# Spreading side work evenly through an attention window, and moving relayout DMAs to another queue

## The chip, the cores and the metric

The kernel runs on one core of a Trainium2 chip. The metric is the device time of one execution in microseconds (us). The trace is of one profiled execution; its span is about 2 to 3 us shorter than the time measured for the same run.

## The reference

CSWin attention over an image of 224 x 224 tokens with 96 channels. A projection gives q, k and v. The first 48 channels attend inside 28 horizontal stripes of 8 rows, the last 48 inside 28 vertical stripes of 8 columns; a stripe ("window" here) has 1792 tokens. Then comes an output projection. Cut to what matters:

```python
qkv = jnp.einsum('bhwc,cd->bhwd', x, wqkv)            # x (1,224,224,96), wqkv (96,288), bfloat16
qh = q[..., :C2].reshape(B * nh, sw * W, C2)          # 28 horizontal windows, C2 = 48
ah = _softmax(jnp.einsum('bqc,bkc->bqk', qh, kh) * scale, axis=-1)
oh = jnp.einsum('bqk,bkc->bqc', ah, vh).reshape(B, H, W, C2)
# the same over 28 vertical windows, with transposes before and after, gives ov
o  = concat(oh, ov)                                   # written with two pads and a sum
return jnp.einsum('bhwc,cd->bhwd', o, wo)
```

## The kernel before

The kernel writes one program per engine. A window is 25 groups: 24 of two 128x512 score tiles, each followed by one 128x1024 exp on ScalarE (ACT), and one half group. The score matmuls of group G wait until exp has freed the PSUM banks of group G-2, so PE and ACT share two PSUM buffers. The products with V (PV) follow two or three groups later.

Everything else PE has to do for a window is a queue of "side items": four transposes of x, eight q and k projections and two of v, 14 in all, for the next window; in vertical windows also four transposes (ot) and four output projections (fin). After every even group, two items are taken from the queue. PE's program has its work in this order.

```python
        while True:
            cur_slot["G"] = G
            if G < NG:
                g = groups[G]
                if g["first_of_win"]:
                    ...                               # load x of window wid + 2
                    if wid + 1 < NWIN:
                        enqueue_proj(wid + 1)         # 14 items
                emit_st(G)                            # scores on PE, exp on ACT
            if G % 2 == 0 or G >= NG:
                for Gp in (G - 3, G - 2):
                    if 0 <= Gp < NG and Gp not in pv_cnt:
                        emit_pv(Gp)
                emit_from(2)                          # two side items, while there are any
            G += 1
```

The DMAs between the two layouts go through DRAM. POOL issues them and waits for each; SP issues the loads and stores. The weights arrive in one tile, and POOL copies them into padded ones.

```python
        def pool_dma(out_ap, in_ap):
            pool.wait(pq_sem, pq_sem.cnt)             # one relayout at a time
            return dma(pool, pq_sem, out_ap, in_ap)

        dma(act, w_sem, wst[:, :], wqkv[:, :])
        dma(act, w_sem, wo_sb[:, :], wo[:, :])
        pool.wait(w_sem, c_w)
        ...                                           # ten tensor_copy on POOL: wst -> wq, wk, wv
        c_pool_const = pool.op(lambda e: e.memset(sigt[:, 0:1], 1.0), sig=True)   # PE waits for this
        ...
        src = xf[L * w: L * (w + 1)].rearrange("(b p) c -> p b c", p=128)         # x rows of 192 B
```

At the change from horizontal to vertical (the "transition"), the last horizontal result goes to DRAM, is relaid out there, and comes back as Ocomb, for which the first ot item waits.

The softmax here doesn't subtract the row's maximum and nothing guards it: scores larger than these inputs give would overflow.

## Time and profile before

Median 1359.84 us over five runs (1357.71 to 1361.52). The profiled run spans 1356.8 us.

| what | before |
|---|---|
| ACT busy | 1280.4 us, 94% |
| PE busy | 1134.5 us, 84% |
| exp: idle before it, ended by PE | 62.8 us |
| DMA share | about 22% |
| one horizontal window | 24.07 us |
| one undisturbed vertical window | 22.91 us |
| recorded time at half PE clock | 245 us in 28 stretches |

From the page of the kernel before: busy time of each engine; then, over 40 equal slices, busy tenths of ACT and the PE clock that was granted, also in tenths; then the shares of the chain that ended last.

```profile
PE 1134.5 (84%) x16918; PEld 617.0 (45%) x16918; DVE 586.8 (43%) x1456; ACT 1280.4 (94%) x1401; POOL 56.1 (4%) x141
...
ACT  5999999999999999999989999999999999999996
PEclk9887898899889788888967999999999989999998
...
ACT 81%; PE 17%; DMA 1%; issue 1%; DVE 0%; POOL 0%; ACTq 0%; POOLq 0%; DVEq 0%
```

ACT sets the time, and the chain says so too. But the horizontal half, the left half of the slices, has clocks of 7, 8 and 9 tenths where the vertical half has 9 nearly throughout.

Next, the largest groups of instructions of the kernel before: line, engine, operation, output from input, count | busy us, mean ns | idle time before, and what ended it.

```profile
L525 ACT ACTIVATE PT<-ps 128x1024 bf16<-128x1024 f32 x1344 | 1251.6, 1055 | 64.9 <-PE ps L514 62.8
L514 PE MATMUL ps<-QT,KT 49*128 49x512 bf16 (+1 forms) x3136 | 571.9, 389 | 207.1 <-ACT PT L525 196.0
...
L126 POOL DMA_DIRECT2D oh_scratch<-oh_scratch x28 | 18.8, 673 | 593.2 <-DMA oh_scratch<-O_sb 593.2
L126 POOL DMA_DIRECT2D out_dram<-out_scratch x28 | 15.4, 549 | 634.3 <-DMA out_scratch<-out_sb 612.5
```

Of the 64.9 us in which ACT stood before an exp, PE's scores ended 62.8. POOL's relayouts have 593 and 613 us of waiting ahead of them, but the chain that ended last puts 0% of the span down to POOL.

Where the idle time lies is seen in ACT's own timeline, here from the kernel before around one end of a horizontal window (start us, length us, what, [idle before <- what ended it]).

```profile
205.78 1.94 ACT L525 ACTIVATE PT<-ps 128x1024 bf16<-128x1024 f32 x2 [0.20 <-PE ps L514]
207.61 0.60 ACT L527 ACTIVATE PT<-ps 128x512 bf16<-128x512 f32 x1
208.42 1.02 ACT L525 ACTIVATE PT<-ps 128x1024 bf16<-128x1024 f32 x1 [0.21 <-PE ps L514]
210.64 1.94 ACT L525 ACTIVATE PT<-ps 128x1024 bf16<-128x1024 f32 x2 [1.20 <-PE ps L514]
213.07 1.94 ACT L525 ACTIVATE PT<-ps 128x1024 bf16<-128x1024 f32 x2 [0.49 <-PE ps L514]
```

The stretch view of the same place in the kernel before has the clock: stretch, its length, busy us of PE, PEld, DVE, ACT and POOL, granted PE clock, DMA share, GB/s.

```profile
202.00:203.00 1.00, 0.98 (x20) 0.63 (x20) 0.00 (x0) 1.00 (x2) 0.00 (x0) 1.00 0.05 16
203.00:204.00 1.00, 0.47 (x6) 0.13 (x4) 0.00 (x0) 1.00 (x2) 0.00 (x0) 0.90 0.00 0
204.00:206.00 2.00, 2.00 (x28) 0.98 (x24) 0.00 (x0) 1.80 (x3) 0.00 (x0) 0.50 0.00 0
...
212.00:214.00 2.00, 2.00 (x24) 1.10 (x23) 1.02 (x2) 1.50 (x3) 0.00 (x0) 0.50 0.13 21
214.00:216.00 2.00, 1.90 (x31) 0.93 (x28) 1.29 (x2) 2.00 (x4) 0.67 (x1) 0.99 0.21 32
```

The rest follows from the order of emission. Fourteen items at two per even group are gone after seven even groups; in the second half of a horizontal window PE has only scores and PV. Depending on how that falls on the grid, a grid window comes out low enough for a drop (in the 19 drops of the horizontal phase the grid window before had PE busy for 0.677 to 0.715). The next attention window then begins with two items per even group at half clock, and there PE can't keep up with ACT: from 212 to 214 us PE is busy for 2.00 us of 2.00, ACT for 1.50.

### The profile page before, as it was taken

The page shows a single profiled execution, that of the slowest core. Times are in us where ns is not written, and L with a number is a line of the kernel's source. Part 1 is how long each engine was busy: PE and PEld are TensorE (multiplying, and loading weights), DVE is VectorE, ACT ScalarE, POOL GpSimd, SP SyncE. Part 2 cuts the span into 40 slices and gives each one's busy share as a digit, 9 for nine tenths or more (in the row PEclk, how much of TensorE's full clock was granted, in tenths as well). Part 3 has the DMA queues.
Part 4 walks back from the last instruction along what each step waited for, and adds up shares of the span by engine and source line. Part 5 has one row for each costly group of instructions (what it writes and reads, how often), then busy time and mean ns, then how long its engine had stood idle before and what let it go on. Part 6 is the DMA issues. An engine that isn't in the chain of part 4 may idle for free.

```text
span 1356.8 us, 37466 instructions
## 1 busy us (share of the span) xinstructions
PE 1134.5 (84%) x16918; PEld 617.0 (45%) x16918; DVE 586.8 (43%) x1456; ACT 1280.4 (94%) x1401; POOL 56.1 (4%) x141
## 2 busy tenths in 40 slices
PE   7888878878887888888889888888888888888886
PEld 3444444444444444444445444444444444444443
DVE  3443333424334343343434555555554545455552
ACT  5999999999999999999989999999999999999996
POOL 1000000000000000000000000000000000000000
PEclk9887898899889788888967999999999989999998
DMA  2221222212122221222222222222222222222211
GB/s 36 45 49 33 49 46 44 49 39 56 34 49 47 43 49 34 50 44 45 50 43 50 57 54 57 53 54 48 56 54 55 50 53 57 52 55 53 57 33 34
DMA packets 263408, 65.07 MB, mean 48 GB/s; under 512 B 257512, under 2 KB 257608, under 8 KB 263248
## 3 DMA queue, kind: packets, MB, share of 16 engines
q1 hardware_dynamic: 255872, 38.56, 16.5%
q0 software_dynamic: 7152, 24.04, 6.1%
q8 instruction: 132, 2.16, 0.7%
q14 instruction: 28, 0.23, 0.1%
q10 hardware_dynamic: 224, 0.07, 0.0%
HBM read 48.19 MB, written 38.49 MB: 64 GB/s over the span
## 4 chain that ended last, share of the span: by engine, by line
ACT 81%; PE 17%; DMA 1%; issue 1%; DVE 0%; POOL 0%; ACTq 0%; POOLq 0%; DVEq 0%
ACT PT L525 80%; PE ps L514 7%; PE ps L560 5%; PE ps L274 2%; PE ps L299 1%; PE ps L348 1%; ACT PT L527 0%; DMA Ocomb<-oh_scratch 0%; DMA oh_scratch<-oh_scratch 0%; DMA wo_sb<-in_wo_dram 0%; PE ps L375 0%; DVE KT L307 0%; DMA out_scratch<-out_sb 0%; DMA oh_scratch<-O_sb 0%; DVE QT L307 0%
## 5 line engine op out<-in xcount | busy, mean ns | idle before, releaser
L525 ACT ACTIVATE PT<-ps 128x1024 bf16<-128x1024 f32 x1344 | 1251.6, 1055 | 64.9 <-PE ps L514 62.8
L514 PE MATMUL ps<-QT,KT 49*128 49x512 bf16 (+1 forms) x3136 | 571.9, 389 | 207.1 <-ACT PT L525 196.0
L560 PEld LDWEIGHTS ps<-VA,PT 128*128 128x128 bf16 x10976 | 347.5, 99 | 193.6 <-issue 183.7
L560 PE MATMUL ps<-VA,PT 128*128 128x49 bf16 x10976 | 426.2, 190 | 0.9 <-DVE VA L330 0.6
L514 PEld LDWEIGHTS ps<-QT,KT 49*128 49x128 bf16 x3136 | 137.5, 95 | 521.5 <-ACT PT L525 427.3
L581 DVE RECIPROCAL rl<-ps 128x4 f32<-128x4 f32 x224 | 40.3, 180 | 357.9 <-PE ps L560 357.9
L307 DVE CAST QT<-ps 128x512 bf16<-128x512 f32 x224 | 135.7, 617 | 64.6 <-PE ps L299 64.6
L307 DVE CAST KT<-ps 128x512 bf16<-128x512 f32 x224 | 138.4, 618 | 25.2 <-PE ps L299 25.0
L281 DVE COPY xT<-ps 96x512 bf16<-96x512 bf16 x224 | 84.8, 382 | 69.0 <-PE ps L274 68.7
L355 DVE COPY OTs<-ps 96x512 bf16<-96x512 bf16 x112 | 43.4, 387 | 122.1 <-PE ps L348 122.1
L274 PE MATMUL ps<-ident,xin 128*96 128x128 bf16 x784 | 92.9, 253 | 0.0
L383 DVE CAST out_sb<-ps 128x384 bf16<-128x384 f32 x112 | 56.7, 506 | 79.7 <-PE ps L375 79.2
L299 PE MATMUL ps<-xT,wk 96*128 96x512 bf16 x224 | 83.6, 373 | 2.1 <-POOL sigt L154 1.2
L274 PEld LDWEIGHTS ps<-ident,xin 128*96 128x96 bf16 x784 | 72.8, 149 | 7.1 <-issue 4.6
L299 PE MATMUL ps<-xT,wq 96*128 96x512 bf16 x224 | 75.9, 361 | 0.0
L330 DVE CAST VA<-ps 128x384 bf16<-128x384 f32 x112 | 56.2, 502 | 28.7 <-PE ps L321 28.7
L348 PE MATMUL ps<-ident,Ocomb 128*96 128x128 bf16 x392 | 44.7, 234 | 1.9 <-DMA Ocomb<-oh_scratch 1.9
L126 POOL DMA_DIRECT2D oh_scratch<-oh_scratch x28 | 18.8, 673 | 593.2 <-DMA oh_scratch<-O_sb 593.2
L597 DVE TENSOR_TENSOR O_sb<-ps,rl 128x192 bf16<-128x192 f32 x112 | 37.3, 333 | 11.9 <-DVE rl L581 0.5
L126 POOL DMA_DIRECT2D out_dram<-out_scratch x28 | 15.4, 549 | 634.3 <-DMA out_scratch<-out_sb 612.5
L597 DVE TENSOR_TENSOR Ocomb<-ps,rl 128x192 bf16<-128x192 f32 x112 | 37.2, 332 | 3.9
L321 PE MATMUL ps<-wv,xT 96*128 96x48 bf16 x784 | 37.9, 184 | 0.5 <-DVE xT L281 0.5
(28 smaller groups left out, 224.3 us busy)
## 6 DMA issues: line engine op xcount, KB each, us to landing
x_scratch<-in_x_dram POOLq DMA_DIRECT2D x28, 336.0 KB, 3.4
xin<-x_scratch SPq DMA_DIRECT2D x28, 336.0 KB, 3.8
xin<-in_x_dram SPq DMA_DIRECT2D x27, 336.0 KB, 3.8
out_dram<-out_scratch POOLq DMA_DIRECT2D x27, 336.0 KB, 3.2
out_scratch<-out_sb SPq DMA_DIRECT2D x84, 96.0 KB, 1.9
oh_scratch<-oh_scratch POOLq DMA_DIRECT2D x28, 168.0 KB, 2.8
Ocomb<-oh_scratch SPq DMA_DIRECT2D x28, 168.0 KB, 2.8
oh_scratch<-O_sb SPq DMA_DIRECT2D x84, 48.0 KB, 1.8
```

The lines of the kernel that those rows point to most:

```text
L274: c = pe.op(lambda e, bb=bb, blk=blk, bank=bank, s=s: e.transpose(psb[0:96, 1024 * bank + 128 * bb: 1024 * bank + 128 * (bb + 1)], xin[s][ ...
L281: cd = dve.op(lambda e, bank=bank, b=b, q0=q0, wdt=wdt: e.tensor_copy(xT[b][:, q0:q0 + wdt], psb[0:96, 1024 * bank: 1024 * bank + wdt]), s ...
L299: c = pe.op(lambda e, bank=bank, b=b, q0=q0, wdt=wdt, wmat=wmat: e.matmul(ps[:, 512 * bank: 512 * bank + wdt], wmat[:, :], xT[b][:, q0:q0 ...
L307: cd = dve.op(lambda e, bank=bank, dst=dst, q0=q0, wdt=wdt: e.tensor_copy(dst[:, q0:q0 + wdt], ps[:, 512 * bank: 512 * bank + wdt]), sig=True)
L330: cd = dve.op(lambda e, bank=bank, b=b, blk0=blk0, nb=nb: e.tensor_copy(VA[b][:, blk0: blk0 + nb, 0:48], ps[:, 512 * bank: 512 * bank + 48 ...
L348: c = pe.op(lambda e, bank=bank, qb=qb, vb=vb, j=j: e.transpose(psb[0:96, 1024 * bank + 128 * qb: 1024 * bank + 128 * (qb + 1)], Ocomb[vb] ...
L355: cd = dve.op(lambda e, bank=bank, vb=vb, q0=q0, wdt=wdt: e.tensor_copy(OTs[vb][:, q0:q0 + wdt], psb[0:96, 1024 * bank: 1024 * bank + wdt] ...
L383: cd = dve.op(lambda e, bank=bank, vb=vb, j=j, nqb=nqb: e.tensor_copy(out_sb[vb][:, 4 * j:4 * j + nqb, :], ps[:, 512 * bank: 512 * bank + ...
L514: c = pe.op(lambda e, base=base, bk=bk, col=col, width=width, rt=rt, i=i, b=b, q0=q0: e.matmul(ps[:, base + 512 * bk + col: base + 512 * b ...
L525: ca = act.op(lambda e, base=base, pt=pt: e.activation(pt[:, 0:1024], ps[:, base:base + 1024], ACTF.Exp, scale=scale), sig=True)
L560: c = pe.op(lambda e, obank=obank, jj=jj, pt=pt, pcol=pcol, qb=qb, b=b, i=i, st=st: e.matmul(ps[:, 512 * obank + 64 * jj: 512 * obank + 64 ...
L597: c2 = dve.op(lambda e, so=so, nqb=nqb, oview=oview, dst=dst: e.tensor_tensor(dst, oview[:, :, 0:48], rl[so][:, 0:nqb].unsqueeze(2).broadc ...
```

## The change

Its summary names DMAs: move the relayout DMAs from POOL to SP, load the weights into their padded tiles directly, put the horizontal relayouts off by a window so that SP doesn't block. The diff has two further parts: x rows are laid out so that a partition reads 2688 contiguous bytes in horizontal windows, and the number of side items per even group is computed. One warm-up matmul is added too. Its core, cut:

```diff
-KNOBS = dict(nwh=28, nwv=28, warm=6, dummies=0)
+KNOBS = dict(nwh=28, nwv=28, warm=7, dummies=0)
...
-        dma(act, w_sem, wst[:, :], wqkv[:, :])
-        ...                                          (ten POOL copies)
+        for d0 in (0, 64):
+            dma(act, w0_sem, wk[0][:, d0:d0 + 48], wqkv[:, 96:144])
+        for d0 in (0, 64):
+            dma(act, w0_sem, wq[0][:, d0:d0 + 48], wqkv[:, 0:48])
+        dma(act, w0_sem, wv[0][:, :], wqkv[:, 192:240])
...
-            return dma(pool, pq_sem, out_ap, in_ap)
+            return dma(sp, rq_sem, out_ap, in_ap)
...
-                    src = xf[L * w: L * (w + 1)].rearrange("(b p) c -> p b c", p=128)
+                srcw = xf[L * w: L * (w + 1)].rearrange("(p b) c -> p b c", b=NKB)
...
                 if j == 3:
-                    pool_after_hwin(wid)
+                    if w == NWH - 1:
+                        flush_pending_hwin()
+                        sp_after_hwin(wid)
+                    else:
+                        pending_hwin.append(wid)     (flushed after chunk 0 of the next window)
...
-                emit_from(2)
+                if G < NG:
+                    gl = G % NGW
+                    even_left = max(1, (NGW - gl + 1) // 2)
+                    nelig = sum(1 for ent in queue if ent[2] <= G)
+                    k = (nelig + even_left - 1) // even_left
+                    k = max(1, min(3, k))
+                else:
+                    k = 2
+                emit_from(k)
```

The last hunk shares the waiting items out over the even groups left in the window: in a horizontal window 2,(2),1,1,...,1 in place of 2,2,2,2,2,2,2,0,0,0,0,0.

## The prediction

> **What bounds the kernel.** ScalarE. The page's busy table gives ACT 1280 of 1357 us (94%); the chain of waits runs 80% over the exp (ACT PT). Back to back, a 128x1024 exp takes 0.927 us, a window (24 and a half one) 22.9 us. ACT's timeline shows 24.07 us per window in the horizontal phase (39.8 to 689.7 us, 27 windows), but 22.91 in clean vertical windows. The surplus is ACT waiting for PE ps L514.

> **Why PE is late.** The stretch view shows PEclk falling to 0.50 28 times, 244 us in all, in whole multiples of 3.41 us on one fixed grid. [...] On that grid nearly every full-clock window with PE busy below about 0.71 is followed by a drop (27 drops, busy 0.57 to 0.715; 296 kept windows average 0.83). Before emits two side items (transposes, projections) per even group until the 14 of a horizontal window are gone; from group 14 on PE has only scores and PV (1.35 us busy per 1.84 us pair, 0.73), on the threshold. About every second window drops (203.8 to 214.0 us), and the next window's front-loaded items run at half clock: ACT loses 0.2+0.2+1.2+0.5 us.

> **What the change does, by worth.**
> 1. Adaptive emission. Counting through the queue: horizontal windows go from 2,2,2,2,2,2,2,0,0,0,0,0 to 2,(2),1,1,1,...,1. One item (0.36 to 0.40 us) per pair lifts PE to about 0.85. Horizontal drops should nearly vanish: 27 x (24.07 - 22.91) = 31 us. In the vertical phase the empty slots at window ends are filled too; drops there cost about 6.8 us, I count 5.5.
> 2. Transition (690 to 744 us): two windows take 54.2 instead of 45.8 us: a drop on entry, 1.85 us of PE waiting for Ocomb, then seven low-clock grid windows. The change removes the entry drop (1.9 us) but keeps the chain store, relayout, Ocomb load, now with the last x relayout inside the wait. I expect a stall of about 2 us again, and half clock after it: 2 us net.
> 3. Relayouts from POOL to SP: the POOL waits (612 and 593 us) are off the critical path; DMA is at about 22%. [...] about 0, with SP not blocking loads because the waits are deferred a window. Contiguous x rows (2688 rather than 192 B) cut packets: about 0 too.
> 4. Direct weights: removes copies ending at 5.5 us (PE waited 1.2 us for sigt); five ACT issues at 0.47 us plus 2.4 us landing give an estimated 5.2 us; one more warm matmul (0.43 us) delays the transposes. Net within 0.5 us.

> Sum: 31 + 5.5 + 2 = 38.5 us, all on the critical path.

> **Predicted:** 1321 us, range 1312 to 1338. Faster by over 2%: 0.86, within 2%: 0.12, slower: 0.02.

> **What would show it right:** 22.9 to 23.0 us per horizontal window; mean PEclk from 0.91 to about 0.98; low stretches from 244 us to under 60, mostly around the transition and the end; no idle before exp at window starts; POOL nearly idle; q0 software packets gone, q1 packets well down.

> **What would make it wrong:** PE with one item per pair still near the threshold (drops moved, not removed); a thinly loaded PE recovering more slowly; the SP queue, now in order for everything, delaying a load; a longer Ocomb stall; three-item slots late in vertical windows; weight loads contending with the first x loads.

31 + 5.5 + 2 = 38.5 us, off the 1359.84 us of before, is 1321 us. The "about 0" of point 3 stands on what the page of before shows: POOL's 612 and 593 us of waiting off the chain, and a DMA share of about 22%. "The threshold" is the busy share of about 0.71 read from the trace of before.

## The result, and the profile after

The kernel after takes 1318.0 us (median of 8 runs, 1311.55 to 1320.78), before 1357.86 us (15 runs). The ratio is 0.9699, 95% interval 0.9682 to 0.9716: 3.0% faster. A ratio here is the mean time of one kernel's runs over that of the other's of the same rounds, so it isn't quite the ratio of the medians quoted. All results below are correct.

The same lines of the page, for the kernel after:

```profile
PE 1053.8 (80%) x16919; PEld 577.9 (44%) x16919; DVE 591.1 (45%) x1456; ACT 1273.3 (97%) x1401; POOL 1.8 (0%) x19
...
ACT  5999999999999999999989999999999999999997
PEclk6999999999999999999979999999999999999998
...
ACT 89%; PE 8%; DMA 1%; DVE 1%; issue 0%; ACTq 0%; SPq 0%; DVEq 0%
```

ACT is at 97% and carries 89% of the chain, the clock row is all nines but for the start, the transition and the end. PE is busy for 81 us less, though it does the same work and one matmul more: its mean granted clock is 0.979 and not 0.910, and a score matmul takes 364 ns on average and not 389. POOL has next to nothing left to do. Recorded low clock: 56 us in 8 stretches, of which 20 in the first 28 us, which the trace of before does not record.

The groups of the kernel after that answer to those of before (its POOL groups are too small for the list):

```profile
L564 ACT ACTIVATE PT<-ps 128x1024 bf16<-128x1024 f32 x1344 | 1244.7, 1080 | 28.7 <-PE ps L553 28.3
L553 PE MATMUL ps<-QT,KT 49*128 49x512 bf16 (+1 forms) x3136 | 540.6, 364 | 245.9 <-ACT PT L564 239.7
```

The ACT timeline of the kernel after, from the end of one horizontal window over the next one to the start of the one after that:

```profile
85.36 0.78 ACT L566 ACTIVATE PT<-ps 128x512 bf16<-128x512 f32 x1
86.14 22.14 ACT L564 ACTIVATE PT<-ps 128x1024 bf16<-128x1024 f32 x24
107.97 0.80 ACT L566 ACTIVATE PT<-ps 128x512 bf16<-128x512 f32 x1
108.76 1.02 ACT L564 ACTIVATE PT<-ps 128x1024 bf16<-128x1024 f32 x1
110.06 2.85 ACT L564 ACTIVATE PT<-ps 128x1024 bf16<-128x1024 f32 x3 [0.27 <-PE ps L553]
```

The waits at the end of a window are gone but for 0.27 us once in two windows. Idle before exp fell from 64.9 to 28.7 us. ACT's busy time fell too, by 7 us: an exp that stands alone is counted with 1.02 us, one in an unbroken row with 0.92 (22.14 us for 24), so a break in the row is partly counted as busy.

Where the 44.1 us between the two profiled spans come from, read at the same exps in both ACT timelines (the profiled run of after was 2 us below its median):

| stage | before | after | difference |
|---|---|---|---|
| start to first exp of the second window | 39.77 | 40.55 | +0.8 |
| 27 horizontal windows from there | 649.9 (24.07 each) | 617.5 (22.87 each) | -32.4 |
| the two windows of the transition | 54.2 | 50.6 | -3.6 |
| 26 vertical windows, to the end of the last exp | 603.3 | 596.6 | -6.7 |
| from there to the end | 9.7 | 7.5 | -2.2 |

### The profile page after: what moved, and what is told of

Read it like the earlier page. It is cut to its first block, busy times and chain, and to the rows that moved or that the text cites. A ratio compares the mean times of both kernels' runs of the same rounds, so it can differ in the third digit from the quotient of the medians.

```text
span 1312.7 us, 37516 instructions
## 1 busy us (share of the span) xinstructions
PE 1053.8 (80%) x16919; PEld 577.9 (44%) x16919; DVE 591.1 (45%) x1456; ACT 1273.3 (97%) x1401; POOL 1.8 (0%) x19
## 2 busy tenths in 40 slices
DMA packets 195287, 65.09 MB, mean 50 GB/s; under 512 B 172504, under 2 KB 191672, under 8 KB 195128
## 4 chain that ended last, share of the span: by engine, by line
ACT 89%; PE 8%; DMA 1%; DVE 1%; issue 0%; ACTq 0%; SPq 0%; DVEq 0%
ACT PT L564 89%; PE ps L553 3%; PE ps L599 3%; PE ps L291 1%; PE ps L373 1%; PE ps L320 1%; ACT PT L566 1%; DMA x_scratch<-in_x_dram 0%; DMA wv<-in_wqkv_dram 0%; DMA Ocomb<-oh_scratch 0%; DVE KT L328 0%; ACTq L124 0%; DMA oh_scratch<-O_sb 0%; PE ps L346 0%; DVE QT L328 0%
## 5 line engine op out<-in xcount | busy, mean ns | idle before, releaser
L564 ACT ACTIVATE PT<-ps 128x1024 bf16<-128x1024 f32 x1344 | 1244.7, 1080 | 28.7 <-PE ps L553 28.3
L553 PE MATMUL ps<-QT,KT 49*128 49x512 bf16 (+1 forms) x3136 | 540.6, 364 | 245.9 <-ACT PT L564 239.7
L599 PE MATMUL ps<-VA,PT 128*128 128x49 bf16 x10976 | 401.0, 185 | 0.9 <-DVE VA L355 0.6
L599 PEld LDWEIGHTS ps<-VA,PT 128*128 128x128 bf16 x10976 | 325.1, 96 | 161.6 <-issue 157.0
L620 DVE RECIPROCAL rl<-ps 128x4 f32<-128x4 f32 x224 | 40.2, 180 | 162.4 <-PE ps L599 162.4
L320 PE MATMUL ps<-xT,wk 96*128 96x512 bf16 x224 | 80.1, 358 | 2.3 <-DMA wv<-in_wqkv_dram 1.4
L320 PE MATMUL ps<-xT,wq 96*128 96x512 bf16 x224 | 80.2, 359 | 0.0
L291 PE MATMUL ps<-ident,xin 128*96 128x128 bf16 x784 | 79.0, 224 | 0.0
L291 PEld LDWEIGHTS ps<-ident,xin 128*96 128x96 bf16 x784 | 58.8, 125 | 3.6 <-issue 0.9
L566 ACT ACTIVATE PT<-ps 128x512 bf16<-128x512 f32 x56 | 39.8, 710 | 0.0
L418 PE MATMUL ps<-wo_sb,OTs 96*128 96x96 bf16 x392 | 35.0, 205 | 1.0 <-DVE OTs L380 1.0
```

The lines of the kernel that those rows point to most:

```text
L291: c = pe.op(lambda e, bb=bb, blk=blk, bank=bank, s=s: e.transpose(psb[0:96, 1024 * bank + 128 * bb: 1024 * bank + 128 * (bb + 1)], xin[s][ ...
L320: c = pe.op(lambda e, bank=bank, b=b, q0=q0, wdt=wdt, wmat=wmat: e.matmul(ps[:, 512 * bank: 512 * bank + wdt], wmat[:, :], xT[b][:, q0:q0 ...
L553: c = pe.op(lambda e, base=base, bk=bk, col=col, width=width, rt=rt, i=i, b=b, q0=q0: e.matmul(ps[:, base + 512 * bk + col: base + 512 * b ...
L564: ca = act.op(lambda e, base=base, pt=pt: e.activation(pt[:, 0:1024], ps[:, base:base + 1024], ACTF.Exp, scale=scale), sig=True)
L566: ca = act.op(lambda e, base=base, pt=pt: e.activation(pt[:, 0:512].rearrange("p (b n) -> p b n", b=2), ps[:, base:base + 1024].rearrange( ...
L599: c = pe.op(lambda e, obank=obank, jj=jj, pt=pt, pcol=pcol, qb=qb, b=b, i=i, st=st: e.matmul(ps[:, 512 * obank + 64 * jj: 512 * obank + 64 ...
```

## The experiments

The theory: PE's granted clock. The spread items keep PE's busy share above the 0.71 or so below which the trace of before has its drops, and all else in the change is worth next to nothing. The rivals: (R1) the gain comes from the DMA side: relayouts off POOL, fewer packets, direct weights; (R2) it comes from spreading as such: bursts of two items make PE late at any clock, and the low clock is a by-product. (In some expectations a name for what sets the clock is cut, in that of e5 with its level of 0.71 busy, and in that of e10 a forecast of PE's load in the prologue: that a drop follows from a low busy share is the author's theory from the trace of before, and no run shows by what means.)

### Alone and undone: e1 and e2

e1 is the kernel before with the last hunk of the diff alone. e2 is the kernel after with that hunk taken back:

```diff
-                ... k = max(1, min(3, k)) ...
-                emit_from(k)
+                emit_from(2)
```

> The kernel before with the adaptive emission count alone; relayouts stay on POOL, x rows stay 192 B, weights are copied by POOL. Spreading theory [...]: nearly all of the gain, ratio 0.970 to 0.974 to before (1317 to 1323 us), low-clock time under 70 us of before's 244. Rival (the moved relayouts, fewer packets and idle POOL carry the gain): ratio above 0.985 (over 1338 us).

> The kernel after with the fixed two items per even slot put back; all DMA and weight changes stay. Spreading theory: back to before, ratio 0.995 to 1.003 (1352 to 1362 us), low-clock time over 200 us. Rival (DMA side carries the gain): ratio below 0.985.

Measured: e1 1318.65 us, ratio 0.9721 (0.9699 to 0.9743), low clock for 40 us. e2 1356.73 us, ratio 0.9998 (0.998 to 1.0016), low clock for 257 us. (The traces of before, e1, e3, e5 and e9 have no record of the clock in the first 26 to 28 us, those of after, e2, e6, e7 and e8 have 20 us of low clock there: compare the sums with that in mind.) From the page of e1, the clock row; from its groups, exp:

```profile
PEclk9999999999999999999989999999999999999999
L525 ACT ACTIVATE PT<-ps 128x1024 bf16<-128x1024 f32 x1344 | 1245.2, 1079 | 30.5 <-PE ps L514 29.8
```

The same of e2:

```profile
PEclk6987888899878879889978999999999999999998
...
L564 ACT ACTIVATE PT<-ps 128x1024 bf16<-128x1024 f32 x1344 | 1251.5, 1056 | 65.8 <-PE ps L553 63.2
```

So the emission hunk carries the gain, and the whole DMA side, which gave the change its name, is worth nothing that these intervals can tell from zero. R1 falls. The DMA side did what it says: POOL busy from 56.1 to 1.8 us, DMA packets from 263408 to 195287. Of the chain, POOL has 0% and DMA 1% in both. The parts of the DMA side were not run one by one, so e2 speaks for their sum alone.

In the traces the DMA side seems to have two small effects that partly cancel. The end is shorter: last exp to end takes 9.7 us in before and 9.6 in e1, where POOL issues the last relayout, and 7.5 in after and 7.6 in e2, where SP does. (Not always: e9 below, with SP, has 9.4 us, since its last store to DRAM took 3.8 us to land and not 1.9. How much of the difference is the issue itself was not measured apart.) The start may be longer: the second window begins at 39.8 and 39.6 us with the old weights, at 40.6 and 40.7 with the new. But over all traces except that of e10, whose edit is aimed at the start, the old ones give 39.1 to 40.4 and the new ones 40.1 to 40.9, so this difference is hardly clear of the scatter.

### Low clock or bursts: e3 and e5

e3 keeps the items of the kernel before where they are, bursts of two and all, and fills each empty even group with one matmul that nobody reads:

```diff
-                emit_from(2)
+                nq = emit_from(2)
+                if nq == 0 and G < NG:
+                    bank = misc_bank()
+                    pe.op(lambda e, bank=bank: e.matmul(
+                        ps[:, 512 * bank: 512 * bank + 512], ident[:, :], warm[:, 0:512], start=True, stop=True))
+                    misc_done(misc_state["dve_hist"][-1])
```

(The tile warm is set to 1.0 for this.) e5 is the same with 128 columns in place of 512.

> The kernel before with its front-loaded items left where they are, and in each even slot that emits no item one 512-column matmul nobody reads. It does more PE work than before. [...] (PE too idle in the empty slots, so its clock halves): the horizontal drops go, ratio about 0.970 to 0.978, horizontal window 22.8 to 23.0 us. Rival (front-loading itself is what makes PE late, at any clock): no gain or a loss, ratio 0.995 or more, because the bursts of two items stay and more work is added.

> As e3 (before plus a dummy matmul in each empty even slot), but with a quarter of the columns, 128. [...] a quarter dummy lifts the slack windows from 0.68 only to about 0.71, so some but clearly fewer drops than before: low-clock time between 40 and 160 us, ratio 0.975 to 0.990. If a dummy helped in any other way than by PE's busy share (say by breaking up waits), its length should not matter: ratio as e3's, 0.967, and low-clock time under 25 us.

Measured: e3 1312.91 us, ratio 0.9674 (0.9654 to 0.9695). It does 182 matmuls more than the kernel before and is as fast as the kernel after or faster, a little more of a gain than the 0.970 to 0.978 that was expected. Its low clock sums to 15 us: one stretch at the transition, one near the end, and the end itself. The horizontal window is 22.81 us. e5 took 1341.81 us, ratio 0.9862 (0.9824 to 0.9901), with 138 us of low clock. Stretch view of e3 for two parts of the horizontal phase, with the clock at 1.00 in both:

```profile
60.00:250.00 190.00, 156.91 (x2445) 80.76 (x2444) 73.05 (x184) 188.56 (x209) 9.72 (x16) 1.00 0.23 47
250.00:656.00 406.00, 335.46 (x5217) 171.66 (x5216) 156.29 (x390) 403.65 (x446) 21.87 (x36) 1.00 0.22 47
```

The same of e5, where the clock is 0.93 and 0.91 (in before 0.86 over 60 to 250 us and 0.87 over 250 to 680):

```profile
60.00:250.00 190.00, 156.19 (x2362) 82.64 (x2359) 71.27 (x176) 183.50 (x203) 9.75 (x16) 0.93 0.22 45
250.00:650.00 400.00, 331.97 (x4977) 176.18 (x4973) 150.83 (x374) 386.23 (x425) 20.72 (x34) 0.91 0.22 46
```

R2 falls: at full clock the bursts of two items cost nothing that shows (a horizontal window takes 22.81 us in e3 with seven of them, 22.87 in after with two at most). And the length of the dummy matters as a threshold in PE's busy share would have it. In e5, apart from the start, the stall at the transition and the end, the full-clock grid windows that dropped had PE busy from 0.660 up to 0.692, and the lowest that kept the clock had 0.688. The two ranges overlap, and in other runs more so. Over all twelve traces, without the first 30 and the last 60 us of each, 91 of 111 full-clock grid windows with PE busy below 0.70 were followed by a drop, 29 of 148 between 0.70 and 0.72, and 4 of 3837 above that, the highest at 0.730 in e4. So the drops go closely with the busy share that the trace gives, but not exactly, and what sets the clock is not shown.

### One phase alone: e4

The kernel before with the adaptive count in horizontal windows only (`if G < NGW * NWH`).

> The kernel before with the adaptive count in the horizontal windows alone. Spreading theory: the horizontal gain of about 29 to 31 us stays, the vertical one of 5 to 6 us is missing: ratio 0.975 to 0.980, one-window drops at vertical window ends as in before. Rival (the gain is in the vertical phase or at the transition): ratio above 0.985.

Measured: 1325.92 us, ratio 0.9767 (0.9746 to 0.9788), as expected. Eight drops of one grid window each are in its vertical phase, where the kernel after had none before the last window. So about 7 us of the gain are vertical, the rest horizontal and at the transition.

### What the kernel after still loses: e6, e7, e8

In the kernel after, PE still waits for the relayout chain at the transition, as predicted. ACT timeline of after, at the first vertical window:

```profile
659.34 5.61 ACT L564 ACTIVATE PT<-ps 128x1024 bf16<-128x1024 f32 x6 [0.27 <-PE ps L553]
665.56 3.77 ACT L564 ACTIVATE PT<-ps 128x1024 bf16<-128x1024 f32 x4 [0.62 <-PE ps L553]
671.56 1.94 ACT L564 ACTIVATE PT<-ps 128x1024 bf16<-128x1024 f32 x2 [2.23 <-PE ps L553]
674.06 4.00 ACT L564 ACTIVATE PT<-ps 128x1024 bf16<-128x1024 f32 x4 [0.56 <-PE ps L553]
```

The 2.23 us at 671.6 us are the wait for Ocomb as ACT feels it; the smaller waits behind it, of which one is shown, lie in the low stretch from 670.0 to 680.2 us. The 0.62 us at 665.6 us come from another drop, of one grid window from 663.2 us, before the stall.

e6 holds the first ot and fin items back by four groups; e7 takes one item in place of two at a window's first group; e8 adds a 512-column dummy wherever fewer than two items are emitted.

```diff
 e6
+                late = 4 if (wid == NWH and j == 0) else 0
-                enqueue_prio(("ot", wid, j), (...), G + 2)
-                enqueue_prio(("fin", wid, j), (...), G + 4)
+                enqueue_prio(("ot", wid, j), (...), G + 2 + late)
+                enqueue_prio(("fin", wid, j), (...), G + 4 + late)
 e7
                     k = max(1, min(3, k))
+                    if gl == 0:
+                        k = 1
 e8
-                emit_from(k)
+                ne_ = emit_from(k)
+                if ne_ < 2 and 0 < G < NG:
+                    ...                              (the dummy of e3)
```

> The kernel after with the first output transpose of the first vertical window held back by four groups, so that it no longer meets the DMA chain store, relayout, Ocomb load. Theory (the stall makes PE idle 1.7 us and that costs the clock for three further grid windows): stall gone, no drop at 670 us, 3.5 to 4.5 us off: ratio to before about 0.967 where the kernel after has 0.970. Rival (the drop at the transition comes from the thin schedule, not from the stall): stall gone, drop stays, at most 2 us off.

> The kernel after with one item instead of two in the slot at a window's first group, where exp waits 0.27 us once per two windows. Theory (the two transposes behind the short exp make PE late): the 0.27 us gaps go, 28 of them, about 6 to 7 us off: ratio about 0.965. Rival (less PE work at the window's start only puts another grid window under the threshold): gaps go, but new drops come, ratio 0.969 or more.

> The kernel after, plus one 512-column dummy in each even slot that emits fewer than two items. [...] the five one-window drops left in the horizontal phase go as well, 2 to 5 us off: ratio 0.966 to 0.969, low-clock time outside prologue and end under 15 us. Rival (more PE work now delays exp): ratio above 0.972 and more exp idle than the 28 us of the kernel after.

Measured: e6 1312.11 us, ratio 0.9658 (0.9638 to 0.9678). No wait for Ocomb is left and no drop at the transition, and its two windows take 45.85 us in place of 50.6. The same place in e6:

```profile
660.11 1.02 ACT L564 ACTIVATE PT<-ps 128x1024 bf16<-128x1024 f32 x1
661.41 21.22 ACT L564 ACTIVATE PT<-ps 128x1024 bf16<-128x1024 f32 x23 [0.27 <-PE ps L553]
682.48 0.64 ACT L566 ACTIVATE PT<-ps 128x512 bf16<-128x512 f32 x1
683.27 22.20 ACT L564 ACTIVATE PT<-ps 128x1024 bf16<-128x1024 f32 x24 [0.16 <-PE ps L553]
```

The stall and not the thin schedule cost the three grid windows of low clock behind it. (That the drop of 663.2 us is missing too can't be put down to the edit: e1 and after, with the same emission, have five and three single drops in the horizontal phase.) e7 1309.78 us, ratio 0.9635 (0.9614 to 0.9656): the 0.27 us waits are gone in both phases, and its trace has a single drop in the horizontal phase, not more. Its rival, that less work at the window's start costs new drops, falls.

e8 1316.05 us, ratio 0.9685 (0.9667 to 0.9703). All drops of the horizontal phase are gone, low clock outside start and end is 6.8 us. Yet the gain over the kernel after is within the intervals. Two horizontal windows take 45.92 us in e8 and 45.59 us in after: 24 exps in a row take 22.21 us in place of 22.14, and the rest is lost between the rows. Here, where after had few drops left (four of one grid window up to the transition), filling every group cost about what it brought. Why a row lasts longer in e8 these runs don't tell. PE's load alone doesn't explain it: e3 has PE busier than after over 60 to 250 us (156.9 against 147.6 us), and its rows of 24 take 22.13 us there.

### Together: e9 and e10

e9 is e6 and e7 in one. e10 adds, to e9: a semaphore for each of the first three weight matrices, so that k's projection needn't wait for v's weights; a few dummy matmuls behind the first items of the prologue; and one item at a window's last group.

```diff
+        keep = {("xt", 0, 0): 3, ("q", 0, 0): 5, ("xt", 0, 1): 2, ("k", 0, 1): 2, ("xt", 0, 2): 2, ("xt", 0, 3): 2}
         def _emit_entry(ent):
             ...
+            for _k in range(keep.get(key, 0)):
+                pe.op(lambda e: e.matmul(ps[:, 512 * 5:512 * 6], warm[:, 0:128], warm[:, :], start=True, stop=True))
...
             if ph == 0:
-                pe.wait(w0_sem, c_w0)
+                pe.wait(w0_sem if which == "q" else wk0_sem, 32)
...
-                    if gl == 0:
+                    if gl in (0, NGW - 1):
                         k = 1
```

> The kernel after with e6 (first output transpose held back) and e7 (one item at a window's first group) together. If the two are independent, their gains add: about 4 and 8 us off the kernel after, ratio to before 0.960 to 0.962 (1303 to 1307 us). If both drew on the same loss: ratio not below 0.963.

> e9, with a semaphore for each of the three first weight matrices, dummy matmuls behind the first projection items, and one item at a window's last group too. Theory: k starts about 1 us earlier, [...] the second window starts at 36 to 39 us rather than 40.2 us, the 0.16 us gaps of the vertical phase go: 3 to 6 us off e9, ratio 0.956 to 0.959. Rival (the prologue waits for VectorE copies, dummies only delay it): prologue as long or longer, ratio as e9's or worse.

Measured: e9 1305.51 us, ratio 0.961 (0.9593 to 0.9628); the two gains add, as far as the intervals tell. e10 1297.76 us, ratio 0.9566 (0.955 to 0.9582): 4.3% faster than the kernel before, and about 20 us by the medians below the kernel after; off e9 it is 7.8 us, where 3 to 6 were expected. In e10 the k projection starts at 5.15 us (6.13 in after), the second window at 36.3 us (40.1 in e9), and idle before exp is down to 12.8 us. Its start has 6.8 us of recorded low clock, after's 20.5. The three parts of e10 weren't run one by one. ACT timeline of e10 in the prologue, where the first exp starts at 7.44 us (8.62 in after) and the second window with the row of 24 at 36.34:

```profile
7.44 2.14 ACT L569 ACTIVATE PT<-ps 128x1024 bf16<-128x1024 f32 x2 [3.00 <-PE ps L558]
10.58 1.02 ACT L569 ACTIVATE PT<-ps 128x1024 bf16<-128x1024 f32 x1 [1.01 <-PE ps L558]
12.36 1.97 ACT L569 ACTIVATE PT<-ps 128x1024 bf16<-128x1024 f32 x2 [0.76 <-PE ps L558]
...
23.73 12.12 ACT L569 ACTIVATE PT<-ps 128x1024 bf16<-128x1024 f32 x13 [0.70 <-PE ps L558]
35.67 0.67 ACT L571 ACTIVATE PT<-ps 128x512 bf16<-128x512 f32 x1
36.34 22.14 ACT L569 ACTIVATE PT<-ps 128x1024 bf16<-128x1024 f32 x24
```

## Why the prediction was right, point by point

The prediction was 1321 us with a range of 1312 to 1338; 1318.0 was measured.

- What bounds the kernel, and why PE is late: right, and shown. e3 removes the drops without moving an item and gains as much as the change; e5 shows that the dose counts.
- 31 us for the horizontal phase: 32.4 by the two traces. 5.5 us for the vertical one: 6.7, together with the tail's drop; e4 gives about 7.
- One item per pair "lifts PE to about 0.85": too high. Over 60 to 250 us of the kernel after, PE is busy 147.56 of 190 us, 0.78. Where the clock is full, a pair has 1.39 us of PE time (groups 5 to 21 of after), against 1.28 us without an item in before: an item adds about 0.1 us to the busy time and not its whole 0.36 to 0.40 us. Added whole, it would even have given over 0.9, so the 0.85 was no sum of the figures beside it. Where the rest of an item goes was not traced. So the margin above 0.71 is thin, as the prediction's first point under what would make it wrong feared, and one-window drops remain at 291, 332 and 561 us; that they are so few was in part luck (e1, with the same emission, has five in the horizontal phase). They are cheap: the attention windows in which they fall are 0.9, 0.7 and 0.7 us longer than their like, against about 2.1 us for a drop in before, likely since the next window no longer starts with a burst. The times of the kernel after scatter over 9 us and those of e3 over 2; that this thin margin is the reason is likely, but not shown.
- The transition: "a stall of about 2 us again", and 2 us net. The stall was 1.7 us; net 3.6 us, since the clock stayed low for three grid windows after the stall, not seven.
- Relayouts and x rows about 0, direct weights "within 0.5 us": right in sum (e2), but not in the parts. The estimate that the weights land at 5.2 us was too early: the last one was issued at 2.68 us and PE could go on at 6.13, about 3.4 us, not 2.4. And the last relayout issued by SP shortens the end by about 2 us in most traces, which I hadn't seen.
- POOL nearly idle, software packets gone, packets well down, low stretches under 60 us, mean clock about 0.98: all came (POOL 1.8 us, no q0 line, 195287 packets, 56 us, 0.979). "No idle before exp at window starts" did not quite come: 0.27 us is left once in two windows, and e7 gains by taking it away.

The low-clock lengths, the busy shares by grid window and the times of windows are sums made from the traces; no view prints them as they stand.

## What to carry to other kernels

Here PE isn't the bottleneck (84% busy in before, ACT 94%), and still its work had to be spread so that every grid window of 3.4 us held enough of it: stretches in which PE was 71% busy on average lost half of the clock 19 times in the horizontal phase of before, and the loss showed up later, where the next burst came. Read the granted clock beside the busy share before anything else, and test a suspicion of the clock with dummy matmuls: that leaves the work itself as it was (e3, ratio 0.9674). Don't judge a change by its title: here the relayouts, weights and packets were worth nothing that shows (e2, ratio 0.9998), and a loop count the gain (e1, 0.9721).
